# Queries and keys in blocks of 256 tokens, empty products first, and the order of the pieces as a table

## The chip, the cores and the metric

The kernel runs on one core of a Trainium2 chip. The core has five engines that each work off a queue of their own, in order: TensorE (PE, with its weight loads PEld), VectorE (DVE), ScalarE (ACT), GpSimd (POOL) and SyncE (SP), which here issues all DMA transfers. Sixteen DMA engines move the data. The metric is the device time of one execution in microseconds (us), as the median of several runs; lower is better.

## What is computed

Two layers follow each other. The first is attention with 8 heads of 64 on 4 sequences of 768 tokens. A token sees the 8 first tokens and the last 96, with a bias that falls with distance by a slope of its own for each head. Its output, 512 wide, goes into a mixture of 4 attention experts; each has its own projections, a causal attention over the whole sequence, and a gate that keeps the best two experts of each token.

```python
def _attn_ref(q, k, v, n_global, n_local) -> np.ndarray:
    B, H, S, D = q.shape
    scale = 1.0 / np.sqrt(D)
    scores = scale * np.matmul(q, k.transpose(0, 1, 3, 2))
    pos = np.arange(S)
    rel = pos[:, None] - pos[None, :]
    is_global = pos[None, :] < int(n_global)
    is_local = (rel >= 0) & (rel < int(n_local))
    keep = is_global | is_local
    dist = np.where(is_global & ~is_local, float(n_local), np.abs(rel).astype(np.float32))
    slopes = 2.0 ** (-8.0 * (np.arange(H, dtype=np.float32) + 1) / H)
    bias = -slopes[:, None, None] * dist[None, :, :]
    scores = scores + bias[None, :, :, :]
    scores = np.where(keep, scores, -1000000000.0)
...
    return np.matmul(a, v).astype(np.float32)
...
    for e in range(E):
        q = x @ wq[e]
        k = x @ wk[e]
        v = x @ wv[e]
        scores = scale * (q @ k.transpose(0, 2, 1))
        causal = np.triu(np.ones((S, S), dtype=bool), 1)
        scores = np.where(causal, -1000000000.0, scores)
...
        ye = a @ v @ wo[e]
        for kk in range(K):
            mask = topk[:, :, kk] == e
            out += mask[..., None] * w[:, :, kk:kk + 1] * ye
```

## The kernel before

The 4 sequences are cut into 24 units of 128 tokens, six to a sequence (`unit(u)`, u from 0 to 23). A unit is a chain of small pieces, each a function that emits a few instructions on one engine; the pieces' names are short and come back in the rows below by the tiles that they write.

First attention. `ldq`, `ldk`, `ldv` (L519) load 128 tokens of each input as 32-bit numbers into `raw`, 256 KB a load; a token's 64 numbers of one head are 256 bytes in one piece. `cq`, `ck`, `cv` (POOL, by the helper `copy`, L358) make 16-bit numbers of them. `tq` (L536) turns queries and keys by 8 transposes on PE, `eq` (DVE) copies them out of PSUM into `qkT`. `s0`, `s1` (L559) are the scores of four heads each against the unit's own and the previous 128 tokens, with keys along the partitions; `x0`, `x1` (ACT, L563) take the exponential, `m0`, `m1` (DVE, L568) multiply by a table `M` that holds bias and mask, `z0`, `z1` (PE, L576 and L579) form the weighted sum with a column of ones for the denominator, and `r` and `n` (DVE, L590, L592) divide. The 8 global keys and values are put over the first 8 rows of the previous tile's keys and values when that tile's own turn is over: `kg`, `kp` (tiles `KG`, `qkT`) and `vg`, `vp` (a small DMA, L600).

Experts. `tx` and `ex` turn the result; `pq` (L618) and `pv` (L624) project it to queries and keys of all experts and to values and gate; `eqk` copies the first out of PSUM into `QK2`, `ev` the values into `V2`; `xr`, `mx`, `wr`, `zi` make the gate. `s2` (L658) and `x2` (ACT, L662) are the scores and exponentials against all tiles so far, `af` (POOL, L670) the causal mask of the newest, `y2` (L682) the weighted sum, `rz`, `cw` (L689), `n2` the division and the gate, `tz`, `ez`, `po` (L705) the output projection, `eo` its copy out of PSUM and `so` (L714) the store of 256 KB.

Buffers are rings: four for `raw`, three for the 16-bit copies, four for most others. PSUM is shared out as two places for scores (`s`) and four for everything else (`w`), and a piece that writes PSUM takes a place from the readers that were there before.

The order on all queues is made when the program is built: `Stream.run` takes, again and again, the piece that a small cost model lets start first, with a rank for each kind of piece (`RANK`) that rises by `PACE` from unit to unit. Pieces that two engines can do (`eqk`, `ev`, `eo`, `m0`, `m1`, `kg`, the weight casts) go to the one that it finds cheaper. At the end a few sums (`good0` to `flag`) look whether all denominators are in range; a general path follows that isn't taken here.

Of the kernel before, what the change touches and what calls it, by code (L numbers as in the profile page):

```python
# [15 lines left out]
HUGE = 1.0e30  # L16
P = 128
N_G, N_L = 8, 96

PACE, ALPHA, TURN = 6.00622, 0.000375979, 0.1
OTHER = {"m0": 3.12, "m1": 3.35, "eqk": 1.71, "ev": 14.02, "eo": 5.29, "kg": -15.22, "kp": 7.23}
RANK = {
# [8 lines left out]
}  # L33
W_RANK = -47.481, 2.337, 16.829, -53.198, 17.758
# [219 lines left out]
class Stream:  # L254
# [4 lines left out]
    def __init__(self, kinds):  # L259
        self.free = {"PE": 0.0, "ACT": 0.0, "DVE": 0.0, "POOL": 0.0, "DMA": 0.0}  # L260
        self.tail = {"PE": 0.20, "ACT": 0.15, "DVE": 0.12, "POOL": 0.10, "DMA": 2.0}
        self.kinds = {k: [()] * n for k, n in kinds.items()}
        self.rows = False
        self.ops, self.done, self.slot = {}, {}, None

    def add(self, key, fn, engines, after=(), rank=0.0, kind=None, until=(), rows=False, stage=None):


        assert key not in self.ops, key
        self.ops[key] = (fn, engines, tuple(after), rank, kind, tuple(until), rows, stage)  # L270

    def ready(self, key):
        fn, engines, after, rank, kind, until, rows, stage = self.ops[key]
        t = 0.0
        for a in after:
            if a not in self.done:
                return None
            t = max(t, self.done[a])
        if kind:

            for r in until:
                if any(a not in self.done for a in self.ops[r][2] if a != key and a not in until):
                    return None
            free = [(max([self.done[a] for a in r], default=0.0), n)
                    for n, r in enumerate(self.kinds[kind]) if all(a in self.done for a in r)]
            if not free:
                return None
            when, self.slot = min(free)
            t = max(t, when)
        return t  # L290

    def run(self):
        left = dict.fromkeys(self.ops)
        while left:
            best = None
            for key in left:
                t = self.ready(key)
                if t is None:
                    continue
                fn, engines, after, rank, kind, until, rows, stage = self.ops[key]  # L300
                for n, (e, length) in enumerate(engines.items()):
# [3 lines left out]
                    if best is None or c < best[0]:  # L305
                        best = c, start, key, e, length, self.slot
# [6 lines left out]
            if e == "PE":  # L313
                self.rows = rows
# [479 lines left out]
```

## Time and profile before

| | |
|---|---|
| median of 3 runs | 157.07 us (156.87 to 157.64) |
| the profiled execution | 157.58 us |
| its span, first to last instruction | 155.8 us |
| DVE busy | 126.7 us (81% of the span) |
| PE busy | 124.4 us (80%) |
| ACT busy | 111.0 us (71%) |
| POOL busy | 72.0 us (46%) |
| DMA engines, the main queue's packets | 77.7% of sixteen engines' span |

The span is what the trace shows; the time of an execution is a little longer, because something lies before the first and after the last instruction. Busy time counts the union of an engine's records. Records of neighbouring instructions overlap a little, so the sum of the records of an engine can be more than its busy time. The PE's ends are modelled, and PE is pipelined, so a busy PE need not be at its peak.

### The profile page before, as it was taken

The numbers are of one execution on the slowest core, as the hardware profiler recorded it, in microseconds if no ns is written. First come the engines' busy times: TensorE is split into PE (matmuls) and PEld (weight loads), VectorE is DVE, ScalarE is ACT, GpSimd is POOL, SyncE is SP. The second block draws the span as 40 slices with busy tenths as digits, with TensorE's granted clock in tenths as the row PEclk, the third lists the DMA queues.
The fourth block names the chain that finished last, engine by engine and source line by source line (L and its number), as shares of the span: only waits on it lengthen the run. The fifth ranks groups of instructions, "written<-read, shape, count | busy, mean of one in ns | idle before, by whom it ended". The sixth has DMA issues, their size and how long they took to land.

```text
span 155.8 us, 5666 instructions
## 1 busy us (share of the span) xinstructions
PE 124.4 (80%) x2246; PEld 99.6 (64%) x2246; DVE 126.7 (81%) x438; ACT 111.0 (71%) x186; POOL 72.0 (46%) x132
## 2 busy tenths in 40 slices
PE   0027885959888988998899989999699999999820
PEld 0015774737777767985777876867588788777400
DVE  3228678987999999898899999999699999978710
ACT  4902457646867987889499968996478879999810
POOL 5037433636476655557938465654392321221000
PEclk9999999999999999999999999999999999999985
DMA  2999669899997999998997999995990221232550
GB/s 52 315 222 215 180 201 231 166 203 234 222 215 137 207 251 217 212 199 172 260 230 206 224 232 199 265 210 144 221 186 4 76 76 67 74 135 74 196 208 13
DMA packets 80687, 27.85 MB, mean 179 GB/s; under 512 B 75632, under 2 KB 77328, under 8 KB 80656
## 3 DMA queue, kind: packets, MB, share of 16 engines
q1 hardware_dynamic: 80656, 27.45, 77.7%
q8 instruction: 18, 0.29, 0.9%
q14 instruction: 13, 0.11, 0.3%
HBM read 20.98 MB, written 6.29 MB: 175 GB/s over the span
## 4 chain that ended last, share of the span: by engine, by line
PE 35%; DVE 21%; DMA 20%; POOL 6%; ACT 5%; issue 5%; SPq 4%; POOLq 0%; ACTq 0%; DVEq 0%
DMA raw<-in_q_dram 13%; DMA raw<-in_k_dram 7%; PE pq L618 6%; DVE A L568 5%; POOL qk L358 5%; PE tq L536 5%; PE po L705 4%; PE z L682 4%; PE s L658 4%; DVE qkT L358 4%; PE pv L624 3%; ACT A L563 3%; PE sc L559 3%; DVE QK L358 2%; DVE cw L689 2%
## 5 line engine op out<-in xcount | busy, mean ns | idle before, releaser
L563 ACT ACTIVATE A<-sc 128x1024 f16<-128x1024 f32 (+1 forms) x48 | 44.8, 962 | 16.0 <-PE sc L559 15.8
L662 ACT ACTIVATE A<-s 128x1024 f16<-128x1024 f32 (+1 forms) x48 | 44.0, 929 | 9.1 <-PE s L658 9.0
L358 POOL CAST qk<-raw 128x512 f16<-128x512 f32 x47 | 31.4, 671 | 31.2 <-DMA raw<-in_q_dram 19.2
L568 DVE TENSOR_TENSOR A<-A,M 128x1024 f16<-128x1024 f16 (+1 forms) x48 | 32.8, 690 | 1.6 <-ACT A L563 1.4
L536 PE MATMUL tq<-ident,qk 128*128 128x128 f16 x192 | 16.1, 231 | 16.3 <-POOL qk L358 15.8
L618 PE MATMUL pq<-xT,wqk 128*128 128x128 f16 x384 | 26.2, 223 | 0.9 <-DVE xT L358 0.7
L670 POOL TENSOR_SCALAR_AFFINE_SELECT A<-A 128x512 f16<-128x512 f16 x24 | 16.8, 699 | 18.8 <-ACT A L662 17.7
L618 PEld LDWEIGHTS <-wqk 128*128 128x128 f16 x384 | 23.1, 100 | 2.6 <-issue 0.9
L536 PEld LDWEIGHTS <-qk 128*128 128x128 f16 x192 | 12.2, 103 | 19.3 <-POOL qk L358 18.1
L358 POOL CAST V<-raw 128x512 f16<-128x512 f32 x24 | 16.2, 675 | 12.2 <-DMA raw<-in_v_dram 6.8
L358 DVE COPY qkT<-tq 128x1024 f16<-128x1024 f16 x24 | 16.3, 678 | 4.1 <-PE tq L536 3.9
L576 PE MATMUL z<-V,A 128*128 128x65 f16 x192 | 17.7, 198 | 2.3 <-POOL V L358 0.9
L592 DVE TENSOR_TENSOR x<-z,rall 128x256 f16<-128x256 f32 x48 | 19.2, 412 | 0.0
L358 DVE CAST QK<-pq 128x512 f16<-128x512 f32 x24 | 16.3, 680 | 1.6 <-PE pq L618 1.6
L658 PE MATMUL s<-QK 64*128 64x128 f16 x336 | 16.2, 218 | 1.3 <-DVE QK L358 1.1
L559 PE MATMUL sc<-qkT 64*128 64x128 f16 x192 | 15.2, 226 | 1.9 <-DVE qkT L358 1.0
L576 PEld LDWEIGHTS <-A 128*128 128x128 f16 x192 | 13.7, 100 | 3.8 <-DVE A L568 1.2
L358 ACT COPY o_sb<-po 128x512 f32<-128x512 f32 x24 | 14.4, 606 | 2.2 <-PE po L705 1.3
L579 PE MATMUL z<-V,A 128*128 128x65 f16 x160 | 14.9, 195 | 0.1
L624 PE MATMUL pv<-wvg,xT 128*128 128x264 f16 x96 | 14.8, 276 | 0.0
L559 PEld LDWEIGHTS <-qkT 64*128 64x128 f16 x352 | 10.9, 97 | 5.9 <-issue 2.8
L705 PE MATMUL po<-wo,zT 128*128 128x512 f16 x48 | 14.3, 380 | 0.3 <-DVE zT L358 0.2
(57 smaller groups left out, 197.9 us busy)
## 6 DMA issues: line engine op xcount, KB each, us to landing
raw<-in_k_dram SPq DMA_DIRECT2D x24, 256.0 KB
raw<-in_q_dram SPq DMA_DIRECT2D x24, 256.0 KB
raw<-in_v_dram SPq DMA_DIRECT2D x24, 256.0 KB
out_dram<-o_sb SPq DMA_DIRECT2D x24, 256.0 KB
w<-in_moe_wq_dram SPq DMA_DIRECT2D x1, 512.0 KB
w<-in_moe_wk_dram SPq DMA_DIRECT2D x1, 512.0 KB
w<-in_moe_wv_dram SPq DMA_DIRECT2D x1, 512.0 KB
wo<-in_moe_wo_dram SPq DMA_DIRECT2D x1, 512.0 KB
```

Of the source, the lines that this page charges most:

```text
L358: act.copy(o, i) if e == "ACT" else (dve if e == "DVE" else pool).tensor_copy(o, i)
L536: nc.tensor.transpose(ps[:, s, p, :], qk16[u % 3][:, s, 2 * p:2 * p + 2, :], ident[:, :])
L559: mm(sc[:, par, pr, prev * P:(prev + 1) * P], lhsT=kt, rhs=qkT[i][L, 0, p, :], start=True, stop=True)
L563: act.activation(A1[(2 * u + hf) % (2 * R)][:, :, :, 0:w], T.pop(("s", u, hf))[:, :, :, 0:w], func=Exp, scale=scale1)
L568: eng[e].tensor_tensor(a, a, M[:, hf, :, :, :] if ri else M0[:, hf, :, :, :], op=Alu.mult)
L576: mm(z[:, h % 4, :], lhsT=a[:, par, pr, 0:P], rhs=V1[i][:, h, 0:DV], start=True, stop=not ri)
L592: add(f"n{hf}", lambda e, hf=hf, r1=r1: dve.tensor_tensor(x16[i][:, 256 * hf:256 * hf + 256].rearrange("p (h d) -> p h d", d=Dh), T.pop((" ...
L618: mm(ps[:, j, :], lhsT=wqk[:, ko, j, :], rhs=xT[i][:, ko, :], start=(ko == 0), stop=(ko == nko - 1))
L624: mm(ps[:, :], lhsT=xT[i][:, ko, :], rhs=wvg[:, ko, :], start=(ko == 0), stop=(ko == nko - 1))
L658: mm(sc[:, par, n, :], lhsT=QK2[b % 2][L, ki, 2 + p2, :], rhs=QK2[b % 2][L, ri, p2, :], start=True, stop=True)
L662: act.activation(A2[i][:, :, 4 * ch:4 * ch + m, :], T.pop(("s2", u, ch))[:, :, 0:m, :], func=Exp, scale=scale2)
L705: mm(ps[:, :], lhsT=zT[i][:, p2, :], rhs=wo[:, p2, :], start=(p2 == 0), stop=(p2 == E // 2 - 1))
```

## The change

Queries and keys are loaded in blocks of 256 tokens, two units at a time. In a partition lie two neighbouring tokens, so that a piece of a load is 512 bytes: 12 loads of 512 KB for queries and 12 for keys in place of 24 and 24 of 256 KB. Values stay as they were. There are three buffers for blocks.

The cast of the queries sorts the two tokens apart; the cast of the keys interleaves the pair, so that two 16-bit numbers make one 32-bit word. Queries are turned by 8 transposes of 16-bit numbers a block, keys by 4 transposes of 32-bit words (`tk`). The query order inside a tile is now all even tokens and then all odd ones; the tables `d` and `M` are built in that order, and `tx` multiplies by a permutation (`perm`) instead of the identity, which puts the tokens back.

Ahead of everything on PE stand 24 products of 128 by 512 zeros (`warm`), whose result is not read.

The planner is gone. `ORDER` is a table of all pieces in the source. A number behind a colon is the PSUM place; a star means the second of the engines that a piece allows. By its stars, `eqk` goes to ACT in 20 of 24 units (before: DVE in all), `ev` to DVE in 7 and `eo` to DVE in 5 (before: ACT in all), and the casts of the first three weights go to ACT (before: DVE). `kg` is on POOL (before: DVE), and the first block's casts are on ACT and DVE.

```diff
+N_WARM = 24
+ORDER = """
+ident nil ldq-0 warm:2 ldk-0 ident32 ldq-2 dg ldk-2 iota d mask ldv-0 d0 d1 M-1-1 ldq-4 cq-0 ck-0
+ld-k M-0-0 M-1-0 tk-0:3 cq-2 tq-0:1 ek-0 ld-q M-0-1 V1one* eq-0 tq-2:2 perm kg-0 s0-0:1 ldv-1 eq-2
...
     def run(self):
...
+        for word in ORDER.split():
+            name, _, slots = word.partition(":")
+            key = names[name.rstrip("*")]
+            fn, engines, after, kind, until = self.ops[key]
+            assert key not in done and done.issuperset(after), word
+            self.slots = [int(n) for n in slots]
+            assert len(self.slots) == len(until), word
+            for n, readers in zip(self.slots, until):
+                assert done.issuperset(self.kinds[kind][n]), word
+                self.kinds[kind][n] = readers
+            fn(list(engines)[name.endswith("*")])
+            done.add(key)
...
+    RB = 3
+    rawqk = ring(RB, [P, 2, H, 2, Dh], F32, "rawqk")
+    rawv = ring(R, [P, H, Dh], F32, "rawv")
+    q16 = ring(RB, [P, 2, H, Dh], FH, "q16")
+    k16 = ring(RB, [P, H, Dh, 2], FH, "k16")
+    qT = ring(RB, [P, H // 2, 2, P], FH, "qT")
+    kT = ring(RB, [P, H // 2, 2, P], FH, "kT")
...
+    def warm(e):
+
+        ps = wtile([P, 4 * P], F32, "warm")
+        for n in range(N_WARM):
+            mm(ps[:, :], lhsT=nil[:, 0:P], rhs=nil[:, :], start=True, stop=True)
...
+        if u == u0:
+            for n, src in enumerate((q, k)):
+                add("ld" + "qk"[n], lambda e, n=n, src=src: nc.sync.dma_start(
+                    rq[:, n, :, :, :].rearrange("p h j d -> p h (j d)"),
+                    src[b, :, ri * P:(ri + 2) * P, :].rearrange("h (p j) d -> p h (j d)", j=2)),
+                    {"DMA": 1.85}, [("c" + "qk"[n], u - 2 * RB)])
+            add("cq", lambda e: copy(e, q_[:, :, :, :], rq[:, 0, :, :, :].rearrange("p h j d -> p j h d")),
+                {"POOL": 0.99} if u else {"ACT": 0.95}, ["ldq", ("tq", u - 2 * RB)], port=True)
+            add("ck", lambda e: copy(e, k_[:, :, :, :].rearrange("p h d j -> p h j d"), rq[:, 1, :, :, :]),
+                {"POOL": 1.27} if u else {"DVE": 0.75}, ["ldk", ("tk", u - 2 * RB)], port=True)
...
+            def tk(e):
+                T["tk", u] = ps = wtile([P, H // 2, P], F32, "tk")
+                for p in range(H // 2):
+                    nc.tensor.transpose(ps[:, p, :], k_[:, 2 * p:2 * p + 2, :, :].rearrange(
+                        "p h d j -> p (h d j)").bitcast(F32), ident32[:, :])
...
-                nc.tensor.transpose(ps[:, ko, :], xv[:, ko, :], ident[:, :])
+                nc.tensor.transpose(ps[:, ko, :], xv[:, ko, :], perm[:, :])
```

The numbers in braces are lengths that the table's author gave the pieces; nothing reads them any more.

On SP's queue the first loads were those of the gate and query weights, then keys and queries of single units (`raw`); before:

```order
L459 DMA wg_68<-in_moe_w_gate_dram 128x16
L459 DMA w_66<-in_moe_wq_dram 128x4x256
L519 DMA raw_82<-in_k_dram 128x8x64
L459 DMA w_66<-in_moe_wk_dram 128x4x256
L519 DMA raw_82<-in_q_dram 128x8x64
L519 DMA raw_83<-in_k_dram 128x8x64
L519 DMA raw_83<-in_q_dram 128x8x64
L519 DMA raw_82<-in_v_dram 128x8x64
```

and after, with blocks of two units (`rawqk`):

```order
L578 DMA rawqk_85<-in_q_dram 128x8x128
L578 DMA rawqk_85<-in_k_dram 128x8x128
L578 DMA rawqk_86<-in_q_dram 128x8x128
L578 DMA rawqk_86<-in_k_dram 128x8x128
L609 DMA rawv_88<-in_v_dram 128x8x64
L578 DMA rawqk_87<-in_q_dram 128x8x128
L512 DMA w_69<-in_moe_wk_dram 128x4x256
L512 DMA w_69<-in_moe_wq_dram 128x4x256
```

The weights have moved behind the first four units' queries and keys, and queries stand ahead of keys.

PE's queue began with the transposes of the first unit (one row of eight is shown of each piece), its scores, and those of the second unit; before:

```order
L536 LDWEIGHTS qk_0_86
L536 MATMUL tq<-ident,qk_0_86 128x128
L559 LDWEIGHTS qkT_89
L559 MATMUL sc<-qkT_89 128x128
...
L536 LDWEIGHTS qk_1_87
L536 MATMUL tq<-ident,qk_1_87 128x128
```

and after (24 empty products, 4 wide transposes, 8 narrow ones of the first block, 8 of the second block, then scores):

```order
L493 LDWEIGHTS nil
L493 MATMUL warm<-nil 128x512
L596 MATMUL tk<-ident_66,k_0_95 128x128 x4
L591 LDWEIGHTS q_0_92
L591 MATMUL tq<-ident,q_0_92 128x2x64
L591 LDWEIGHTS q_1_93
L591 MATMUL tq<-ident,q_1_93 128x2x64
L630 LDWEIGHTS kT_101
L630 MATMUL sc<-qT_98,kT_101 128x128
```

The second block's query transposes stand ahead of the first scores.

On ACT, after the first exponentials of the experts (tile `A<-s`), there stood only exponentials, the value casts (`V`), the cast of the last weights and the output copies (`o_sb`); before:

```order
L662 ACTIVATE A_0_117<-s_359 128x2x256
L563 ACTIVATE A_5_102<-sc 128x1024
L563 ACTIVATE A_4_101<-sc 128x1024
L637 ACTIVATE el_125<-pv 128x4
L358 CAST wo<-wo_67 128x1024
L358 CAST V_0_115<-pv 128x4x64
```

and after:

```order
L731 ACTIVATE A_0_128<-s_458 128x2x256
L634 ACTIVATE A_6_114<-sc 128x1024
L634 ACTIVATE A_0_108<-sc 128x1024
L634 ACTIVATE A_1_109<-sc 128x1024
L384 CAST QK_0_124<-pq 128x512
L384 CAST wo<-wo_70 128x1024
L708 ACTIVATE el_137<-pv 128x4
```

The cast of the projected queries and keys (`QK`) has come onto ACT's queue, from DVE's.

## Rows read from the trace of the kernel before

**Rows 1.** The page's first part: busy us (share of the span) xinstructions.

```profile
PE 124.4 (80%) x2246; PEld 99.6 (64%) x2246; DVE 126.7 (81%) x438; ACT 111.0 (71%) x186; POOL 72.0 (46%) x132
```

**Rows 2.** ACT by stretches: from:to, us, busy us (x), PEclk, DMA share, GB/s.

```profile
0.00:12.70 12.70, 5.44 (x18) 1.00 0.94 198
12.70:30.00 17.30, 9.96 (x15) 1.00 0.86 194
30.00:117.00 87.00, 67.12 (x105) 1.00 0.99 211
117.00:149.80 32.80, 28.44 (x51) 1.00 0.27 100
```

**Rows 3.** DVE by stretches.

```profile
30.00:117.00 87.00, 80.57 (x262) 1.00 0.99 211
117.00:148.50 31.50, 27.86 (x119) 1.00 0.26 93
```

**Rows 4.** PE by stretches.

```profile
10.40:20.70 10.30, 8.37 (x92) 1.00 1.03 218
...
117.00:149.20 32.20, 31.29 (x567) 1.00 0.27 98
```

**Rows 5.** First 24 us in order: start, us, engine, line, what [idle before <-releaser].

```profile
0.93 0.39 SPq L459 DMA_DIRECT2D wg<-in_moe_w_gate_dram  x1
...
1.37 0.42 SPq L459 DMA_DIRECT2D w<-in_moe_wq_dram  x1
...
5.88 0.69 DVE L358 CAST wqk<-w 128x1024 f16<-128x1024 f32 x1 [2.32 <-DMA w<-in_moe_wq_dram]
...
6.96 0.43 DVE L358 CAST qk<-raw 128x512 f16<-128x512 f32 x1 [0.39 <-DMA raw<-in_k_dram]
...
8.54 0.69 DVE L358 CAST wqk<-w 128x1024 f16<-128x1024 f32 x1 [1.15 <-DMA w<-in_moe_wk_dram]
...
9.77 0.61 POOL L358 CAST qk<-raw 128x512 f16<-128x512 f32 x1 [6.55 <-DMA raw<-in_q_dram]
...
10.44 1.04 PE L536 MATMUL tq<-ident,qk 128*128 128x128 f16 x8 [10.44 <-POOL qk L358]
...
12.70 1.09 ACT L563 ACTIVATE A<-sc 128x512 f16<-128x512 f32 x2 [5.14 <-PE sc L559]
...
17.25 1.86 PE L618 MATMUL pq<-xT,wqk 128*128 128x128 f16 x16 [0.52 <-DVE xT L358]
...
23.04 1.05 PE L618 MATMUL pq<-xT,wqk 128*128 128x128 f16 x16
```

**Rows 6.** Groups by shape: busy us, mean ns | idle before, releaser.

```profile
L358 POOL CAST qk<-raw 128x512 f16<-128x512 f32 x47 | 31.4, 671 | 31.2 <-DMA raw<-in_q_dram 19.2 <-DMA raw<-in_k_dram 12.0
...
L592 DVE TENSOR_TENSOR x<-z,rall 128x256 f16<-128x256 f32 x48 | 19.2, 412 | 0.0
...
L358 DVE CAST QK<-pq 128x512 f16<-128x512 f32 x24 | 16.3, 680 | 1.6 <-PE pq L618 1.6
...
L358 ACT COPY o_sb<-po 128x512 f32<-128x512 f32 x24 | 14.4, 606 | 2.2 <-PE po L705 1.3 <-ACT V L358 0.5 <-ACT o_sb L358 0.4
...
L358 ACT CAST V<-pv 128x256 f16<-128x256 f32 x24 | 9.2, 386 | 1.1 <-DVE mx L640 1.0
...
L689 DVE SCALAR_TENSOR_TENSOR cw<-wr,zi,rall 128x4 f32<-128x4 f32 x24 | 7.3, 303 | 0.1
...
L358 DVE COPY KG<-qkT 128x32 f16<-128x32 f16 x4 | 1.7, 429 | 0.1
...
L358 ACT CAST wo<-wo 128x1024 f16<-128x1024 f32 x1 | 1.1, 1067 | 0.0
...
L742 PE MATMUL pf<-ones,good 128*1 128x1 f32 x6 | 0.3, 163 | 0.0
```

**Rows 7.** The tile cw: its product, ns min/median/max.

```profile
L689 DVE SCALAR_TENSOR_TENSOR cw<-wr,zi,rall x24: 193/220/1219, 27.4 to 147.1; 128x4 f32<-128x4 f32 x24
```

More of the change, by code (lines that the diff above doesn't have):

```diff
@@ L259, in __init__, with add @@
     def __init__(self, kinds):
-        self.free = {"PE": 0.0, "ACT": 0.0, "DVE": 0.0, "POOL": 0.0, "DMA": 0.0}
-        self.tail = {"PE": 0.20, "ACT": 0.15, "DVE": 0.12, "POOL": 0.10, "DMA": 2.0}
         self.kinds = {k: [()] * n for k, n in kinds.items()}
-        self.rows = False
-        self.ops, self.done, self.slot = {}, {}, None
-    def add(self, key, fn, engines, after=(), rank=0.0, kind=None, until=(), rows=False, stage=None):
+        self.ops, self.slots = {}, []
+    def add(self, key, fn, engines, after=(), kind=None, until=(), rows=False, port=False):
@@ L269, in add @@
         assert key not in self.ops, key
[L270 to L290, printed above, removed]
@@ L292, in run @@
-    def run(self):
[L293 to L301, printed above, removed]
-                    turn = TURN if e == "PE" and rows != self.rows else 0.0
-                    start = max(t, self.free[e] + turn)
-                    c = start + OTHER.get(stage, 0.0) * n + ALPHA * rank
-                    if best is None or c < best[0]:
-                        best = c, start, key, e, length, self.slot
-            assert best, list(left)[:20]
-            start, key, e, length, slot = best[1:]
-            fn, engines, after, rank, kind, until, rows, stage = self.ops[key]
-            if kind:
-                self.kinds[kind][slot] = until
-                self.slot = slot
-            if e == "PE":
-                self.rows = rows
-            self.free[e] = start + length
-            self.done[key] = start + length + self.tail[e]
-            del left[key]
-            fn(e)
@@ new lines, in add @@
+        self.ops[key] = (fn, engines, tuple(after), kind, tuple(map(tuple, until)))
+    def run(self):
+        names = {"-".join(map(str, k)) if isinstance(k, tuple) else k: k for k in self.ops}
+        done = set()
+        for word in ORDER.split():
[10 more added lines that the diff above has]
+            done.add(key)
+        assert len(done) == len(self.ops)
@@ new lines @@
+    st.add("dg", c_dg, {"POOL": 0.45})
+    st.add("mask", c_mask, {"POOL": 0.9}, ["d"])
+    st.add("d0", dmin(d0[:, :], d[:, 0:P]), {"DVE": 0.35}, ["mask", "dg"])
+    st.add("d1", dmin(d[:, P:2 * P], d[:, P:2 * P]), {"DVE": 0.35}, ["mask", "dg"])
+    for hf in range(2):
+        st.add(("M", 0, hf), c_factor(True, hf), {"ACT": 0.8}, ["d0"])
+        st.add(("M", 1, hf), c_factor(False, hf), {"ACT": 1.25}, ["d1"])
+    st.add("V1one", fill([t[:, :, Dh:DV + 1] for t in V1], 1.0), {"DVE": 0.3, "POOL": 0.3})
@@ L458, in ld @@
+    st.add("V2one", fill([t[:, :, :, Hd:DV] for t in V2], 1.0), {"DVE": 0.3, "POOL": 0.3})
+    st.add("ones", fill([ones[:, :]], 1.0), {"DVE": 0.1})
     def ld(o, i):
@@ L500, in unit, with add @@
         n_ch = (len(ent) + 3) // 4
-        def add(name, fn, engines, after=(), stage=None, kind=None, until=(), rows=False):
+        def add(name, fn, engines, after=(), kind=None, until=(), rows=False, port=False):
             def full(a):
@@ L508, in add @@
                                             (isinstance(x, tuple) and isinstance(x[1], int) and x[1] < u)],
-                   PACE * u + RANK[stage or name], kind, [full(a) for a in until], rows,
-                   stage or name)
+                   kind, [[full(a) for a in one] for one in until], rows, port)
         def c(key):
```

226 lines of the change are left out of this document (144 added, 82 removed), and 8 rows, old and new, of the table RANK.

## The prediction

> **What bounds the kernel now.** I read the busy line of the page first, then each engine's busy time by stretches, then the groups by shape, and the first 24 us instruction by instruction. The page [rows 1] shows no engine at its limit for the whole span: DVE is busy 126.7 us of 155.8, PE 124.4, ACT 111.0. The stretches say why [rows 2 to 4]. From 30 to 117 us the DMA engines are full (share 0.99), and there DVE, the fullest engine, is busy 80.57 us of 87.00, or 93%, ACT only 67.12, or 77%. From 117 on the DMA share is 0.26, since the loads are over, and PE is busy 31.29 of 32.20 us: it works off the second attention that has been left behind. Before 30 us all of them starve: ACT has its first exponential at 12.70 us [rows 5] and is busy 9.96 of the next 17.30 us. So three things set the end, one after the other: a late and thin start, a middle that is held by loads and nearly as much by DVE, and a last stretch on PE.
>
> **The start.** In order of issue before: gate weights, query weights, keys, key weights, queries of the first tile. The query weights (512 KB, pieces of 1 KB) are issued at 1.37 and used at 5.88; then the keys (256 KB, pieces of 256 B) 1.08 us later, the key weights 1.58 us later, the queries 1.23 us later, at 9.77 [rows 5]. So 256 KB in pieces of 256 B cost about 1.15 us (18 ns for each piece and engine, 1024 pieces on 16 engines), and 512 KB in pieces of 1 KB 1.58 us (49 ns a piece). A block of 256 tokens is 512 KB in pieces of 512 B, and no load here has that size. From above it costs 2 x 1.15 = 2.30 us (no gain from the longer piece), from below 1.58 us. On the line between the two pieces one of 512 B takes 28 ns, which makes 1.82 us; I take that, because both ends come from the same queue within 4 us of each other.
> Now the first queries go first: issued at 0.93, where the queue's first load stands [rows 5], 4.5 us from issue to use as the query weights took, 0.24 us more for the smaller pieces, so 5.7 us; the first keys 7.5, the second block's queries 9.3. PE's own queue puts the transposes of that second block's queries ahead of the first scores, so the first scores wait for them: 9.3 + 1.2 to 1.34 us of POOL cast (the cast of half the size takes 0.67 [rows 6]) + 0.6 + 0.3 of PE gives a first exponential at about **11.6 us**, against 12.70. At the upper price of the loads it would be 13.1.
> The 24 empty products need only a memset and lie ahead of everything on PE. What columns cost is seen at 16 products of 128: 1.86 us at 17.25 and 1.05 us at 23.04 [rows 5], 116 and 66 ns each. Four times these bounds the 24 at 6.3 to 11.2 us, so they end between about 8 and 12.5 us; I take 9, as they come without gaps. Up to there they are hidden behind loads that PE waits for anyway; at 12.5 the first exponential would come near 14.5. The granted clock reads 1.00 (the 2.4 GHz level) in the first stretch of PE's work too [rows 4], though the same products take nearly twice as long there as later; PE had done nothing for ten microseconds before it. I go by the durations. PE is busy 8.37 us from 10.40 to 20.70 [rows 4]; at the later price that is 4.7 us, so the warm start takes some 3.6 us off PE, most of it under other engines' waits.
>
> **What each engine has to do.** Counted in the code's tables: of 24 casts of the second attention's queries and keys (QK, 128x512) 20 go from DVE to ACT; 7 value casts and 5 output copies go from ACT to DVE; three weight casts go from DVE to ACT, the four small key copies (KG) from DVE to POOL.
> DVE: 20 x 0.68 off; 7 x about 0.41 (a DVE operation on 256 columns from PSUM) and 5 x 0.68 on; weights 3 x 0.69 and KG 1.7 off; the first key cast and a memset 0.5 on. Together -13.6 + 2.9 + 3.4 - 2.1 - 1.7 + 0.5 = -10.6, so 116.1 us [rows 1, 6]. The 24 copies of the transposed tiles (12 + 12 instead of 24) keep their size and cost.
> ACT: 20 x 0.61 on (the price of the output copy, the same 128x512 from PSUM), 7 x 0.39 and 5 x 0.61 off, 3 x 1.07 of weight casts and one query cast of 1.07 on: 12.2 - 2.7 - 3.1 + 4.3 = +10.7, so **121.7 us** [rows 1, 6]. ACT becomes the fullest engine, and the fullest engine of all falls by only 126.7 - 121.7 = 5.0 us: balance alone gives no more.
> PE: per block 16 transposes of 128 columns become 8, and 4 of 32-bit words. A 32-bit transpose isn't in the trace; the only 32-bit products are recorded as two each (6 for 3 calls) [rows 6]. Eight narrow ones take 1.04 us at 10.44 [rows 5], 0.6 at the later price. Below, 4 wide ones cost as much as 4 narrow (0.3 us); above, four times that, 1.2 us. Against the 8 that they replace this is -0.3 to +0.6 us a block, -3.6 to +6.6 us in 12 blocks; two passes each, as the recorded ones, make 0.6 and no change. I take 0.
> POOL: 47 casts of 0.67 (31.4 us) become 22 of twice the size. At twice the price 29.5 us; the key cast writes every second element, which I bound at one to two times that (29.5 to 44). POOL is busy 72.0 us now and has room. What it can cost is DVE's time: DVE's small product cw takes 193 ns at best and 1219 at worst [rows 7], 303 in the mean [rows 6]. I read the excess, 24 x 0.11 = 2.6 us, as DVE waiting for POOL. Half as many casts of twice the length cover the same time, but each hit lasts twice as long, so the part that the casts cause, 31.4 of POOL's 72.0 us [rows 1, 6], doubles: 1.2 us more on DVE; 0 if the new order keeps the two apart.
> The Trainium skill says the same in its page "SBUF — State Buffer", section "SBUF: two separate sides": the pair of ports that DVE and GpSimd share is an exclusive lock, held for the whole instruction, and the loser blocks fully. By that rule alone the longer casts speak against the change; the worst row [rows 7] agrees, at 1.0 us over the best. What that would make of the time is the rival on POOL's casts below.
> DMA: the loads of queries and keys fall from 48 x 1.15 = 55 us to 24 x 1.82 = 44, so 11.5 us of a stretch that was full until 117 [rows 2]; at the ends of the price 0 to 17. The queue of SP also loses 24 load instructions, but its order is fixed, and a load behind a store that waits for ACT waits too.
>
> **The sum**, along ACT, against the profiled execution's span. First exponential at 11.6. Of ACT's 121.7 us, 5.44 lie before it [rows 2] and 1.07 of query cast: 115.2 remain. Its records overlap a little with their neighbours, so 20 added casts count for about 1 us less: 114.2. The last stretch stays what it was, 28.44 us of work in 32.80 [rows 2], because it hangs on the chain of each last tile and on PE. The other 85.8 us run at the share that the fullest engine reached before, 80.57 of 87.00 [rows 3]: 92.6 us. Then 6.0 us from ACT's last copy to the end (149.80 to 155.80). 11.6 + 92.6 + 32.8 + 6.0 = 143.0. The median stands 157.07 - 155.8 = 1.3 us above the span (the profiled execution itself, 157.58, 1.8). **Forecast 144.3 us.**
> Two checks. DVE: first copy at about 9.6, 116.1 - 1.8 (set-up ahead of it) + 1.2 = 115.5 of work, idle 3.6 in the last stretch (27.86 of 31.50 [rows 3]) and some 4 elsewhere, 7.3 after it: 140.0. PE: from 9, 124.4 - 3.6 = 120.8, idle 5, 6.6 after it: 141.4. All three lie within 3 us of each other, so none of them alone decides, and a saving on one shows little.
>
> **The rivals.**
> *Dense table* (17%). A written order may feed ACT better than 93% without load waits: at 98%, as any engine would with full queues, the middle takes 87.6 us, and the last stretch loses half of its 4.4 idle us: 137.1. For it: the DMA is no longer full. Against it: DVE and PE are as loaded.
> *Three full engines in lockstep* (14%). Each queue is in order; where ACT, DVE and PE all need over 115 us, each waits for the others. At 87% the middle takes 98.6 us: 150.3. The wide or slow 32-bit transposes (+6.6 on PE) and a cold first 10 us (+2.9) lead to the same place.
> *The loads still pace* (6%). If a piece of 512 B costs as much as two of 256 (2.30 us a block), the loads end where they did, and the last stretch follows from 117: up to 157, which is no change; with half of it 152. Against it: 1.58 us for pieces of 1 KB [rows 5].
> *Slower: DVE behind POOL's longer casts* (5%). One mechanism: 24 cw and 48 mask products meet casts of 1.3 us. If each waited 0.3 us more than now (a hit of 1 us, as the worst one shows [rows 7], in every third), DVE has 72 x 0.3 = 22 us more and the check on DVE gives 140.0 + 22 + 1.3 = 163. It decides from 0.23 us on each, 17 us in all. The same row speaks against: median 220 ns against a best of 193, so most meet nothing.
> *It doesn't do what it says* is inside these: if the empty products leave PE no faster, 147.
>
> **How the numbers follow.** Forecast 58%, 140 to 148. Dense 17%, stalls 14%, loads 6% (half of them within 0.5% of 157.07, half faster), POOL 5%. A measurement of this kernel can tell about 0.5% from no change. Faster 0.92, within 0.5% 0.03, slower 0.05. The range leaves out the lowest 5% or so of the dense case and, above, half of the load case, the POOL case and the worst stalls: 138 to 151.
>
> **What would show it.** In the profile after: ACT busy near 121 us and the fullest or next to it, QK casts on ACT at 0.6; DVE near 116; the first exponential at 11 to 12; 16 products of a query and key projection at about 1.0 us from the first; a DMA share clearly under 0.99 in the middle, and loads that end ahead of 110; four 32-bit transposes within 0.6 us. Wrong would be: a middle where ACT is under 87% busy, waits of the score products or of DVE for POOL of over 10 us, a share of 0.99 again, or cw over 500 ns in the mean.

## The result, and the profile after

The changed kernel takes 146.50 us in the median of 4 runs (146.05 to 146.97), against 157.00 before (4 runs, 156.87 to 157.64): a ratio of 0.932, 95% interval 0.929 to 0.936. In a second comparison, beside the experiments, it was 146.34 (ratio 0.923, 0.914 to 0.933). The forecast was 144.3 with a range of 138 to 151; the sign and the range held, and the time is 2.2 us longer than forecast. The kernel before came out at 157.0 to 158.7 in the different comparisons, so each experiment is given with its own ratio to it. Some executions of a kernel, profiled ones among them, fall into a second state that is some per cent slower; medians are of all runs, the ratios of the fast runs alone.

The first part of the page after (busy us, share of the span of 144.9, instructions), then the granted clock and the DMA share by fortieths of the span, the main DMA queue (packets, MB, share of sixteen engines) and the shares of the chain that ended last:

```profile
PE 130.0 (90%) x2222; PEld 101.5 (70%) x2222; DVE 120.2 (83%) x420; ACT 120.1 (83%) x198; POOL 70.2 (48%) x116
...
PEclk9999555999999999999999999999999999999999
DMA  2999999599898997969999699770527204023164
...
q1 hardware_dynamic: 55696, 27.45, 72.2%
...
PE 60%; DVE 14%; DMA 8%; SPq 7%; issue 3%; ACT 2%; POOL 2%; ACTq 0%
```

Against [rows 1] ACT has gained 9.1 us of work (forecast 10.7) and DVE has lost 6.5 (forecast 10.6). PE's 130.0 hold 7.0 us of empty products; without them it has 123.0, 1.4 less than before. The DMA queue moves the same 27.45 MB in 72.2% x 144.9 = 104.6 us of sixteen engines, where it took 77.7% x 155.8 = 121.1.

ACT by stretches (from:to, us, busy us (instructions), granted clock, DMA share, GB/s), the answer to [rows 2]:

```profile
0.00:10.72 10.72, 6.39 (x18) 1.00 0.90 219
10.72:30.00 19.28, 12.60 (x16) 0.73 0.96 254
30.00:117.00 87.00, 80.62 (x128) 1.00 0.81 205
30.00:131.00 101.00, 93.35 (x150) 1.00 0.73 187
131.00:139.90 8.90, 7.01 (x16) 1.00 0.19 71
```

And the same of DVE (first fence) and PE (second fence), the answers to [rows 3] and [rows 4]:

```profile
30.00:98.00 68.00, 63.97 (x207) 1.00 0.94 234
30.00:117.00 87.00, 82.27 (x278) 1.00 0.81 205
30.00:131.00 101.00, 94.34 (x328) 1.00 0.73 187
```

```profile
8.50:30.00 21.50, 15.56 (x208) 0.76 0.99 256
8.50:15.00 6.50, 4.01 (x63) 1.00 1.19 294
15.00:25.00 10.00, 7.92 (x81) 0.50 1.02 253
30.00:117.00 87.00, 84.35 (x1579) 1.00 0.81 205
30.00:131.00 101.00, 98.35 (x1854) 1.00 0.73 187
```

Between 30 and 117 us ACT was busy 77% and is now 93%; DVE went from 93% to 95%, and the DMA engines from 0.99 to 0.81, because most of their work ends earlier: up to 98 us the share is still 0.94, then the DMA row falls to 0. The last load of queries or keys is issued at 85.40 us (before at 110.08); only the last three value loads come after 98 us, the last of them at 109.81. All three engines run at 92 to 97% up to 131 us, and PE has no backlog of the second attention to work off alone: only the last ten microseconds of ACT's work, from 131 us to its last copy's end at 140.7, are thin. The gain lies in the middle; the start is 2 us better, and the end stays an end.

The first 30 us (start, us, engine, line, what), as in [rows 5]:

```profile
1.35 7.02 PE L493 MATMUL warm<-nil 128*128 128x512 f16 x24 [1.35 <-DVE nil L479]
...
6.89 0.77 DVE L384 CAST k<-rawqk 128x1024 f16<-128x1024 f32 x1 [2.61 <-DMA rawqk<-in_k_dram]
...
8.21 0.60 PE L596 MATMUL tk<-ident,k 128*128 128x128 f32 x4
...
8.75 1.04 POOL L384 CAST q<-rawqk 128x1024 f16<-128x1024 f32 x1 [4.81 <-DMA rawqk<-in_q_dram]
...
10.59 1.33 POOL L384 CAST k<-rawqk 128x1024 f16<-128x1024 f32 x1 [0.24 <-DMA rawqk<-in_k_dram]
...
10.72 1.08 ACT L634 ACTIVATE A<-sc 128x512 f16<-128x512 f32 x2 [1.30 <-PE sc L630]
...
18.08 0.69 DVE L384 CAST wvg<-wg 128x16 f16<-128x16 f32 x2 [0.69 <-DMA wg<-in_moe_w_gate_dram]
...
20.17 1.90 PE L689 MATMUL pq<-xT,wqk 128*128 128x128 f16 x16
...
28.84 1.07 PE L689 MATMUL pq<-xT,wqk 128*128 128x128 f16 x16 [1.18 <-DVE z L761]
```

The empty products end at 8.4, and the clock falls all the same: its row reads 1.00 (2.4 GHz) to 15 us, 0.50 (1.2 GHz) from 15 to 25, and 1.00 from there on. The 16 products of the first projection still take 1.90 us, as before.

### The profile page after: what moved, and what is told of

The parts are those of the page before. It is cut to its first block, busy times and chain, and to the rows that moved or that the text cites. A ratio compares the mean times of both kernels' runs of the same rounds, so it can differ in the third digit from the quotient of the medians.

```text
span 144.9 us, 5515 instructions
## 1 busy us (share of the span) xinstructions
PE 130.0 (90%) x2222; PEld 101.5 (70%) x2222; DVE 120.2 (83%) x420; ACT 120.1 (83%) x198; POOL 70.2 (48%) x116
## 3 DMA queue, kind: packets, MB, share of 16 engines
q1 hardware_dynamic: 55696, 27.45, 72.2%
## 4 chain that ended last, share of the span: by engine, by line
PE 60%; DVE 14%; DMA 8%; SPq 7%; issue 3%; ACT 2%; POOL 2%; ACTq 0%
PE pq L689 13%; PE s L727 7%; PE sc L630 7%; PE pv L695 6%; PE z L647 5%; PE z L751 5%; DMA wg<-in_moe_w_gate_dram 5%; PE po L774 4%; SPq L578 4%; DMA rawqk<-in_k_dram 4%; PE tx L679 3%; PE tk L596 3%; DVE A L639 3%; PE z L650 3%; PE tq L591 3%
## 5 line engine op out<-in xcount | busy, mean ns | idle before, releaser
L639 DVE TENSOR_TENSOR A<-A,M 128x1024 f16<-128x1024 f16 (+1 forms) x48 | 35.0, 742 | 0.2 <-ACT A L634 0.2
L384 POOL CAST k<-rawqk 128x1024 f16<-128x1024 f32 x11 | 15.3, 1388 | 12.7 <-DMA rawqk<-in_k_dram 12.6
L630 PE MATMUL sc<-qT,kT 64*128 64x128 f16 x352 | 17.4, 224 | 2.5 <-DVE kT L384 1.2
L647 PE MATMUL z<-V,A 128*128 128x65 f16 x192 | 17.1, 196 | 2.2 <-POOL V L384 1.0
L384 POOL CAST V<-rawv 128x512 f16<-128x512 f32 x24 | 15.7, 658 | 3.9 <-PE s L727 1.9
L647 PEld LDWEIGHTS <-A 128*128 128x128 f16 x192 | 13.1, 99 | 5.1 <-DVE wr L712 0.8
L384 POOL COPY kT<-KG 128x32 f16<-128x32 f16 x20 | 5.4, 272 | 20.9 <-PE sc L630 20.9
L630 PEld LDWEIGHTS <-kT 64*128 64x128 f16 x352 | 11.1, 97 | 5.9 <-issue 1.9
L384 POOL CAST q<-rawqk 128x1024 f16<-128x1024 f32 x11 | 11.7, 1059 | 6.7 <-DMA rawqk<-in_q_dram 6.7
L650 PE MATMUL z<-V,A 128*128 128x65 f16 x160 | 14.6, 195 | 0.0
L384 ACT CAST QK<-pq 128x512 f16<-128x512 f32 x20 | 11.9, 595 | 2.5 <-PE pq L689 2.5
L751 PE MATMUL z<-V,A 128*128 128x65 f16 x336 | 13.8, 193 | 0.0
L751 PEld LDWEIGHTS <-A 128*128 128x128 f16 x336 | 12.3, 97 | 1.8 <-issue 0.4
```

Of the source, the lines that this page charges most:

```text
L384: act.copy(o, i) if e == "ACT" else (dve if e == "DVE" else pool).tensor_copy(o, i)
L630: mm(sc[:, par, pr, prev * P:(prev + 1) * P], lhsT=share(kT, u - prev)[L, p, :], rhs=share(qT, u)[L, p, :], start=True, stop=True)
L639: eng[e].tensor_tensor(a, a, M[:, hf, :, :, :] if ri else M0[:, hf, :, :, :], op=Alu.mult)
L647: mm(z[:, h % 4, :], lhsT=a[:, par, pr, 0:P], rhs=V1[i][:, h, 0:DV], start=True, stop=not ri)
L751: mm(z[:, ex, :], lhsT=A2[i][:, ex % 2, n, :], rhs=V2[b % 2][:, ki, ex, 0:DV], start=(j == 0), stop=(j == len(mine) - 1))
```

## The experiments

Two theories stood at the start. The one of the prediction: more room in the DMA and the shift from DVE to ACT give the gain together, and ACT, DVE and PE then end within 3 us of each other. Rivals: the warm start gives a part of it; the loads' piece size gives nearly all of it; one engine alone is the new bound.

**Without the empty products** (one is left of 24).

```diff
-N_WARM = 24
+N_WARM = 1
```

> The changed kernel with 1 empty product instead of 24 (all else as it is, 146.5 us). Theory (the empty products buy a fast start, but the clock falls back at about 15 us in any case): the first block's transposes and scores take twice as long, first exponential at 11.5 to 12.5 instead of 10.72, the time 147.3 to 148.5. Rival A (nothing is bought, because the clock was at the lower level from 15 to 25 us anyway): 146.1 to 146.9. Rival B (the products at the start only bring a fall at 15 us; without them the clock rises at about 20 us as in the kernel before): 144.5 to 145.8.

Measured: 147.16 us (146.08 to 148.21), ratio 0.931 (0.919 to 0.942), which can't be told from the changed kernel's; it lies between the ranges of the theory and of rival A. The first query transposes and the first projection in this run:

```profile
8.68 2.20 PE L591 MATMUL tq<-ident,q 128*128 128x128 f16 x16
...
20.86 1.90 PE L689 MATMUL pq<-xT,wqk 128*128 128x128 f16 x16
```

The first query transposes take nearly twice as long each here (16 in 2.20 us, against 8 in 0.61 after), so the empty products do speed up PE up to 15 us; the first exponential comes at 11.25 instead of 10.72. Nothing of it is seen at the end.

**More empty products**, 18 in seven groups where PE waits between 11 and 21 us.

```diff
+MORE = {"f0": 2, "f1": 1, "f2": 1, "f3": 3, "f4": 4, "f5": 5, "f6": 2}
...
+    for name, n in MORE.items():
+        st.add(name, more(n), {"PE": 0.215 * n}, ["nil"], "w", [[]])
```

> The changed kernel with 18 more empty products, in 7 groups of 1 to 5, at the places between 11 and 20 us where PE waits. Theory (the ten microseconds at the lower clock level, 15 to 25 us, are dear, because every engine hangs on PE there): the granted clock stays at 1.00 past 15 us, ACT is busy 2 to 4 us more of 10.7 to 30, the time 142.5 to 144.5. Rival (the start is paced by loads and small waits, or the empty products hold up the pieces behind them): 146.0 to 147.5, also where the clock stays up.

Measured: 147.57 us (145.79 to 149.05), ratio 0.925 (0.914 to 0.936). PE in this run from 15 to 20 us, and its first projection:

```profile
15.00:20.00 5.00, 4.21 (x36) 1.00 0.95 259
```

```profile
21.36 1.06 PE L700 MATMUL pq<-xT,wqk 128*128 128x128 f16 x16
```

The clock stays at 1.00 in every fortieth of the span and the 16 products take 1.06 us instead of 1.90, and still the time is the same. Three kernels with three clocks in the first 30 us, one time: PE's clock there is worth less than these comparisons resolve, some 2 us by their intervals. Why is not shown; it may be that until 30 us the engines wait for loads, casts and each other more than for PE. This run is also no clean test of the clock, since its 18 products take time on PE in the same stretch, and its first 24 end at 9.46 us instead of 8.37.

**The empty products alone**, ahead of the kernel before.

```diff
+    def warm(e):
+        ps = wtile([P, 4 * P], F32, "warm")
+        for n in range(24):
+            mm(ps[:, :], lhsT=nil[:, 0:P], rhs=nil[:, :], start=True, stop=True)
```

> The kernel before with only the 24 empty products put at the front of PE's queue (the rest in the same order). Theory (PE's first ten microseconds of work at the lower level cost about 3.6 us of PE, most of it under other waits): 155 to 156.3. Rival (PE idles between the end of the empty products at 8.4 and the first transposes at 10.4 and then works thinly, so that the clock falls again before it helps): 156.5 to 157.5.

Measured: 156.48 us (155.87 to 157.69), ratio 0.988 (0.979 to 0.998). So in the kernel before they gave 0.3 to 3.3 us by the interval, which doesn't decide between theory and rival; the first exponential came at 11.73 instead of 12.70.

**Pieces of 256 bytes again**: the same blocks, tiles and order, but a block's load is two loads that each bring every second token.

```diff
-                add("ld" + "qk"[n], lambda e, n=n, src=src: nc.sync.dma_start(
-                    rq[:, n, :, :, :].rearrange("p h j d -> p h (j d)"),
...
+                add("ld" + "qk"[n], lambda e, n=n, src=src: [nc.sync.dma_start(
+                    rq[:, n, :, j, :],
...
+                    for j in range(2)],
```

> The changed kernel with each load of queries or keys as two loads of 256 KB in pieces of 256 B, the same bytes into the same places. Theory (the longer piece is what makes room on the DMA engines): first exponential 1.0 to 1.5 us later, DMA share of the main queue from 72% to about 80%, more waits of POOL for keys and queries than 19 us, the time 148 to 150.5. Rival (the loads don't pace the new order, only the number of bytes counts): 146.1 to 147.2.

Measured: 156.33 us (154.70 to 157.54), ratio 0.985 (0.975 to 0.996): nearly all of the gain is gone, far more than the theory's 148 to 150.5. Its main queue, then ACT from 30 to 117 us, then what PE and POOL waited for longest (us in total, times, longest):

```profile
q1 hardware_dynamic: 80656, 27.45, 77.0%
```

```profile
30.00:117.00 87.00, 72.55 (x112) 0.98 0.89 202
```

```profile
PE tk L597 <- POOL k L384: 7.0, 7, 2.7
```

```profile
POOL k L384 <- DMA rawqk<-in_k_dram: 20.6, 9, 5.0
...
POOL q L384 <- DMA rawqk<-in_q_dram: 11.8, 7, 6.4
```

In the changed kernel POOL waits 12.6 and 6.7 us for the same loads and PE 0.4 for POOL's keys. The chain is plain: loads, POOL's casts, PE's transposes, and ACT falls from 80.62 to 72.55 us of work in 87. The queue's time is 77.0% x 155.8 = 120.0 us, against 104.6. The Trainium skill, page "DMA: Bandwidth & Descriptors", section "Specifications", gives 512 bytes as the smallest transfer for line rate. The runs agree nearly: the shorter pieces cost 15 us more of the queue's time for the same 27.45 MB, and by the packet records of the kernel after, the median piece takes 18 ns at 256 bytes, 27 at 512 and 49 at 1 KB, so 512 bytes come within a tenth of the rate of 1 KB. One thing isn't told apart: this kernel also issues 24 loads more than the changed one, and the price of those is within the 9 to 10 us.

**All QK casts back on DVE** (20 of them from ACT; all 20 stars, one row is shown).

```diff
-m1-3 eqk-1* tq-6:1 tx-2:0 m1-4 w-o z0-3:2 ex-2 s20-1:1 r0-3 s0-5:0 m0-4 pq-2:0 xr-1 x0-5 wr-1 eq-6
+m1-3 eqk-1 tq-6:1 tx-2:0 m1-4 w-o z0-3:2 ex-2 s20-1:1 r0-3 s0-5:0 m0-4 pq-2:0 xr-1 x0-5 wr-1 eq-6
```

> All 24 QK casts go to DVE again (20 come back from ACT), in the changed kernel's order otherwise: DVE gets 20 x 0.60 = 12 us more, ACT 12 us less. Theory (DVE's work is paid in full, as its doubled copies showed with +6.6 for +6.7): +9 to +12, a ratio to the kernel before of 0.99 to 1.01, and DVE busy 130 to 132. Rival (PE sets the pace, and the relief of ACT gives most of it back): +3 to +6, a ratio of 0.95 to 0.97.

Measured: 155.85 us (155.26 to 156.39), ratio 0.987 (0.977 to 0.997): +9.4, as the theory said, with a ratio a little under its 0.99. The page's busy line and its chain:

```profile
PE 133.1 (86%) x2222; PEld 102.4 (66%) x2222; DVE 131.1 (85%) x440; ACT 112.4 (73%) x178; POOL 69.1 (45%) x116
...
DVE 51%; PE 37%; issue 3%; ACT 3%; POOL 3%; DVEq 0%; ACTq 0%
```

DVE's share of the chain goes from 14% to 51%, and from 30 to 131 us DVE is busy 97.48 of 101 us. With the long pieces but without the shift, DVE is the bound; with the shift but without the long pieces (the run above), the loads are. Each of the two alone is worth little: undoing either one costs 9 to 10 us of a gain of 10.5. One thing stays open here: the table's order was made for these places of the casts, and a move in the other direction costs 3 us too (below), so part of the +9.4 may be the price of a disturbed order. What the order by itself is worth against the planner's was not tested.

**What each engine's work costs now.** Three kernels do one kind of operation twice: the 48 key transposes on PE, 17 value casts on ACT, 24 copies of the transposed second attention (`ez`) on DVE.

```diff
-                for p in range(H // 2):
+                for p in [*range(H // 2)] * 2:
```

> The changed kernel with every transpose of the keys done twice (the same result): 48 more 32-bit transposes, in groups of four that take 0.45 us, so PE has about 5.4 us more, of which 4.5 us lie after 30 us. Theory (PE is what bounds it: 78.8 of 80 us busy from 50 to 130): 4 to 5.5 us longer than the changed kernel on the same chip. Rival (ACT bounds it, as the prediction's sum had it, and PE's records only look full): 0 to 2 us longer.

```diff
-        add("ev", lambda e: copy(e, V2[b % 2][:, ri, :, 0:Hd],
-                                 T["pv", u][:, 0:E * Hd].rearrange("p (e d) -> p e d", d=Hd)),
+        add("ev", lambda e: [copy(e, V2[b % 2][:, ri, :, 0:Hd],
+                                 T["pv", u][:, 0:E * Hd].rearrange("p (e d) -> p e d", d=Hd))
+                             for _ in range(2 if e == "ACT" else 1)],
```

> The changed kernel with the 17 value casts on ACT done twice (the same result): ACT has 17 x 0.38 = 6.5 us more. Theory (PE bounds it and ACT has idle time, 7.7 us of it between 30 and 131 us): 1 to 3 us longer. Rival (ACT bounds it): 4.5 to 6.5 us longer.

```diff
-        add("ez", lambda e: copy(e, zT[i][:, :, :], T.pop(("tz", u))[:, :, :]), {"DVE": 0.2},
+        add("ez", lambda e: [copy(e, zT[i][:, :, :], t[:, :, :]) for t in [T.pop(("tz", u))] * 2], {"DVE": 0.2},
```

> The changed kernel with the 24 copies of zT on DVE done twice (the same result): DVE has 24 x 0.28 = 6.7 us more. Theory (PE bounds it and DVE has some idle time, 4.7 us between 30 and 117 us): 1.5 to 4 us longer. Rival (DVE and its waits for POOL bound it): 5 to 7 us longer.

The changed kernel itself ran beside them:

> The changed kernel itself again, as the base for the kernels sent with it. Its ratio to the kernel before was 0.932; both theories expect 0.925 to 0.94.

| | work added | median | against 146.34 | ratio to before |
|---|---|---|---|---|
| unchanged copy | none | 146.34 | | 0.923 (0.914 to 0.933) |
| PE | 48 transposes, 12 x 0.45 = 5.4 | 150.85 | +4.5 | 0.954 (0.946 to 0.962) |
| ACT | 17 x 0.38 = 6.5 | 149.06 | +2.7 | 0.938 (0.930 to 0.946) |
| DVE | 24 x 0.28 = 6.7 | 152.90 | +6.6 | 0.965 (0.957 to 0.974) |

By the medians, the work added on DVE is paid in full, on PE to some 80%, on ACT to some 40%; each difference is uncertain by 1 to 2 us. DVE's price is the clear one, and the theory that PE alone is the bound falls with it; ACT, along which the prediction made its sum, comes out cheapest. PE's price is less certain than it looks: in the profiled execution (149.99 us, the shortest of the four) ACT's last output copy ends at 141.78 us, against 140.69 in the changed kernel and 139.76 in its copy, so 1.1 to 2.0 us later; the rest of its longer span lies behind that, where a last packet of the stores starts late. The page's busy time doesn't help: without any added work, PE's 2222 products are busy 129.6 us in the copy and 132.0 in the DVE run. And each price is that of one kind of operation at its place in the chain; other operations of the same engine were not tried.

**The twelve value casts and output copies back on ACT** (7 `ev`, 5 `eo`; one row is shown): the test in the other direction, relief for DVE.

```diff
-eo-0 cq-8 ex-3 s21-2:1 s0-7:0 rz-1 x21-2 mx-2 pq-3:2 zi-1 ldv-7 cw-1 x0-7 cv-6 ev-2* wr-2 tq-8:0
+eo-0 cq-8 ex-3 s21-2:1 s0-7:0 rz-1 x21-2 mx-2 pq-3:2 zi-1 ldv-7 cw-1 x0-7 cv-6 ev-2 wr-2 tq-8:0
```

> The 7 value casts and 5 output copies that the change put on DVE go back to ACT, in the changed kernel's order otherwise: DVE 7 x 0.41 + 5 x 0.69 = 6.3 us less, ACT 5.6 us more. Theory (DVE's work counts in full, ACT's at about a third): -6.3 + 2.0, so -3 to -4.5, 142 to 143.5. Rival (PE is as full as DVE, so a relief of DVE alone gives little): -1 to +1, 145.5 to 147.5.

Measured: 149.81 us (149.45 to 151.25), ratio 0.953 (0.942 to 0.963): 3 us slower, where the theory had 3 to 4.5 faster and the rival no change. Both fell. The busy line, and what DVE waited for:

```profile
PE 131.3 (89%) x2222; PEld 102.3 (69%) x2222; DVE 112.7 (76%) x408; ACT 124.2 (84%) x210; POOL 71.3 (48%) x116
```

```profile
DVE wr L712 <- ACT V L384: 4.1, 7, 1.5
...
DVE mx L711 <- ACT el L708: 3.0, 4, 1.4
...
DVE mx L711 <- ACT V L384: 2.3, 3, 1.2
DVE wr L712 <- ACT el L708: 2.0, 4, 0.8
```

In the changed kernel the same waits are 1.0, 2.6, none and 0.2 us. So DVE has 7.5 us less to do and waits 7.6 us more for ACT in these rows: the relief is handed straight to a wait. (All its idle time grows by 10.3 us, from 24.7 to 35.0; what makes up the rest is not shown.) `mx` and `wr` are the gate's small operations on DVE; what they wait for on ACT now stands behind, or is, one of the casts that came back. Taking work off DVE by giving it to ACT is thus no test of DVE alone, and a price found by adding work can't be turned round into a gain.

**The same with the gate weights' load first** on SP's queue.

```diff
-ident nil ldq-0 warm:2 ldk-0 ident32 ldq-2 dg ldk-2 iota d mask ldv-0 d0 d1 M-1-1 ldq-4 cq-0 ck-0
+ident nil ld-g ldq-0 warm:2 ldk-0 ident32 ldq-2 dg ldk-2 iota d mask ldv-0 d0 d1 M-1-1 ldq-4 cq-0 ck-0
```

> As e11_evo, and the load of the gate weights (32 KB) stands first on SP's queue, where it stood in the kernel before, and not behind the loads of the first four blocks, where it landed at 18 us. Theory (the chain of the first gate waits for it): another 0.5 to 1.5 us less than e11_evo. Rival (other waits stand behind that one): no difference, 0 +- 0.5.

Measured: 151.37 us (149.41 to 152.78), ratio 0.950 (0.937 to 0.962) against 0.953 without it: no difference that can be told, as the rival said. It tests little, though: in the run without it the cast of the gate weights starts at 17.98 us with no wait before it, so the wait of 0.69 us that the changed kernel shows at 18.08 wasn't there to be won. (The load has 8 KB, not 32.)

**Half of POOL's casts of queries and keys**, from the fourth block on.

```diff
+            hh = H if u < 2 * RB else H // 2
-            add("cq", lambda e: copy(e, q_[:, :, :, :], rq[:, 0, :, :, :].rearrange("p h j d -> p j h d")),
+            add("cq", lambda e: copy(e, q_[:, :, 0:hh, :], rq[:, 0, 0:hh, :, :].rearrange("p h j d -> p j h d")),
...
-            add("ck", lambda e: copy(e, k_[:, :, :, :].rearrange("p h d j -> p h j d"), rq[:, 1, :, :, :]),
+            add("ck", lambda e: copy(e, k_[:, 0:hh, :, :].rearrange("p h d j -> p h j d"), rq[:, 1, 0:hh, :, :]),
```

> From the fourth block on, POOL casts only half of the heads of queries and keys (the other half of these casts is left out of the computation): POOL has 18 casts of half the length, about 11 us less, and DVE, PE and ACT keep all their work. Theory (POOL's long casts cost DVE time through its waiting): the mask products fall from 797 ns in the mean towards 730, DVE's busy time by 2 to 4 us, the time by 1 to 3. Rival (the casts cost DVE nothing and PE doesn't wait for them): 0 +- 0.7.

Measured: 144.80 us (143.67 to 145.85), ratio 0.915 (0.905 to 0.926): 1.5 us under the changed kernel by the medians, with intervals that overlap by about half. The mask products here and after by min/median/max (ns), and their mean at the full size (busy us, mean ns), after in the first fence of each pair:

```profile
L639 DVE TENSOR_TENSOR A<-A,M x48: 396/681/1762, 11.3 to 126.0; 128x1024 f16<-128x1024 f16 x40, 128x512 f16<-128x512 f16 x8
```

```profile
L640 DVE TENSOR_TENSOR A<-A,M x48: 393/681/1191, 11.4 to 125.2; 128x1024 f16<-128x1024 f16 x40, 128x512 f16<-128x512 f16 x8
```

```profile
L639 DVE TENSOR_TENSOR A<-A,M 128x1024 f16<-128x1024 f16 x40 | 31.5, 797 | 0.0
```

```profile
L640 DVE TENSOR_TENSOR A<-A,M 128x1024 f16<-128x1024 f16 x40 | 29.8, 754 | 0.0
```

The median stays and the worst falls by 0.57 us. What makes a product long is seen in the changed kernel's own trace, where one begins 0.02 us after a cast on POOL:

```profile
42.33 1.56 DVE L639 TENSOR_TENSOR A<-A,M 128x1024 f16<-128x1024 f16 x1
```

```profile
42.31 1.04 POOL L384 CAST q<-rawqk 128x1024 f16<-128x1024 f32 x1 [0.31 <-DMA rawqk<-in_q_dram]
```

The product ends 0.54 us after the cast. So do the others: of the 40, the 15 that overlap nothing on POOL take 652 to 693 ns, and the eleven over 700 ns all begin while a cast or a causal mask (`af`) is running on POOL and end 0.49 to 0.55 us after it. A product thus waits for what is left of POOL's instruction. The nine that overlap a cast of queries or keys make up 3.3 of the 4.6 us that the 40 take above the median; value casts and POOL's masks make up the rest.

What shorter casts bring is small: 40 x 43 ns = 1.7 us of DVE's time, of which the second profile of the changed kernel (mean 770) leaves 0.6, because value casts and masks then hit more. DVE's busy time is 118.5 us, 1.7 or 0.4 less than in the changed kernel's two profiles, where the theory had 2 to 4. That the kernel is faster by 1 to 3 us is not shown.

## Why the prediction was right, and where not

**The shape was right.** Three limits one after the other; the loads leave the middle, the work goes from DVE to ACT, and ACT, DVE and PE stand together. The two runs that undo one side each (256-byte pieces, QK casts on DVE) show the two limits that the profile before named, 0.99 of the DMA and 93% of DVE: lift one alone and the other one holds nearly the old time.

**The sum along ACT** gave 144.3, and it hides errors that partly cancel:

| term | forecast | measured | difference |
|---|---|---|---|
| first exponential | 11.6 | 10.72 | -0.9 |
| ACT's work from there on | 114.2 | 113.7 | -0.5 |
| ACT's idle time up to its last copy | 6.8 + 4.4 = 11.2 | 6.7 + 7.6 + 1.9 = 16.2 | +5.0 |
| from there to the span's end | 6.0 | 4.2 | -1.8 |
| outside the span | 1.3 | 1.6 | +0.3 |

The idle time is the mis-sized term. It was taken as one share, 93%, from the first exponential on; that share came true from 30 to 117 us (80.62 of 87.00), but the first 19 us after the first exponential run at 65%, 12.60 of 19.28, hardly better than before (9.96 of 17.30). The stage before 30 us should have been a term of its own, as the tail was. That the total came within 2.2 us owes something to luck, since the start, ACT's work and the end of the span were each over-estimated, by 3.2 us together. That the last stretch would stay as it was, 28.44 in 32.80, was wrong too, though it cost the sum little: with the loads out of the way earlier, PE keeps pace with the other engines up to 131 us.

**The start.** The order of the loads did what was forecast: keys used at 6.89 (7.5), the second block's queries at 8.75 (9.3). The empty products end at 8.4 (9). That they "take some 3.6 us off PE" was wrong: they hold the upper level of the clock to 15 us only, PE without them is busy only 1.4 us less than before, the first projection's 16 products took 1.90 us where 1.0 was given as a sign, and the runs with one, with 24 and with 42 take the same time. The remark on the rivals that the time is 147 if the empty products leave PE no faster comes nearest to what was seen.

**DVE and ACT.** ACT's 121.7 came out as 120.1, the moved QK casts at 595 ns each. DVE's 116.1 + 1.2 came out as 120.2, 3 us more. Of that, the mask products account for 2.7 (40 at 797 ns in the mean, 730 before; 1.6 by the second profile's 770), and this is in the main the term of POOL's longer casts, forecast at 1.2: I looked for it at the wrong tile. `cw`, by which it was priced, did not rise at all (mean 269, median 223, worst 975 ns, against [rows 7]). The mask products before, then `cw` after:

```profile
L568 DVE TENSOR_TENSOR A<-A,M 128x1024 f16<-128x1024 f16 x40 | 28.9, 730 | 1.0 <-ACT A L563 0.9
```

```profile
L758 DVE SCALAR_TENSOR_TENSOR cw<-wr,zi,rall x24: 191/223/975, 27.3 to 138.0; 128x4 f32<-128x4 f32 x24
```

The Trainium skill's rule that GpSimd and a DVE operation with two SBUF inputs lock a port pair against each other for the whole instruction (page "SBUF — State Buffer", section "SBUF: two separate sides") is borne out by the overlaps shown for the run with half the casts: the products over 700 ns end 0.49 to 0.55 us after the POOL instruction during which they began. The price that would have made the change slower, 0.23 us on each of 72 operations or 17 us, was not near: the mean rose by 67 ns on the 40 full mask products and fell on the 24 `cw`.

**POOL.** Its 22 casts were forecast at 29.5 to 44 us and came out a little under, at 11 x 1388 + 11 x 1059 ns = 26.9 us: twice the size costs less than double for queries (1059 against 2 x 671) and about double for the interleaved keys.

```profile
L384 POOL CAST k<-rawqk 128x1024 f16<-128x1024 f32 x11 | 15.3, 1388 | 12.7 <-DMA rawqk<-in_k_dram 12.6
...
L384 POOL CAST q<-rawqk 128x1024 f16<-128x1024 f32 x11 | 11.7, 1059 | 6.7 <-DMA rawqk<-in_q_dram 6.7
```

**PE's 32-bit transposes.** Taken at no change against the eight that they replace: four take 0.60 us together at 8.21, and doubling them added 0.43 to 0.48 us in each of the first three blocks. The bound of +6.6 us, four times a narrow one each, was far off; the pass count of the only other 32-bit product in the trace pointed the right way.

**The DMA.** Forecast 11.5 us less of the loads, with ends of 0 and 17; measured 121.1 - 104.6 = 16.5, near the upper end. The price of the new piece was right: its packets take 27 ns in the median (28 forecast, on the line between 18 and 49), and the second block's queries and keys are used 1.86 and 1.84 us after the block loaded just ahead of them, where 1.82 was taken. What was mis-sized is the old loads, priced from the first few alone. Over the whole run a 256-byte packet took 20.4 ns in the mean before, so that 48 loads took 62.7 us of sixteen engines and not 55; a 512-byte packet took 31.7 after, so that 24 blocks took 48.7 and not 44. That is 14.0 us of the 16.5; the rest is mostly value loads and stores, whose packets became a little quicker.

**The rivals.** The dense table (137.1) did not come: ACT stayed at 92 to 93% in the middle, where PE's records fill 97%. The loads would have paced at 152 to 157 had the piece not become cheaper: the run with 256-byte pieces measured 156.3. The lockstep of three full engines (150.3) came in part, as the 5 us of idle time more and as the relief of DVE that ended in a wait for ACT. That none of the three alone decides fits the runs; the choice of ACT for the sum was not a good one: work added on ACT cost some 40% of its length, work added on DVE all of it.

## What to carry to other kernels

Where two limits lie close together (here a full DMA and an engine at 93%), price an edit that lifts both as one thing: undoing either half gave back nearly the whole gain, so the halves must not be added up or tried singly and dropped. Before work is moved between two engines that are both over 90% busy, look at what stands behind it in the receiver's queue and who waits for that, since the giver's relief may come back as a wait of the same size. And doubling one cheap operation on each engine gives a first idea of whose time is paid for, which the busy shares (90, 83 and 83%) did not: DVE's came out dearest and ACT's cheapest. It is a price at that place in the chain, and not one for the whole engine.

## What was not expected of the hardware

The record of the granted clock doesn't tell the first level. With one empty product it reads 1.00 in every fortieth of the span, yet 16 transposes took 2.20 us at 8.68 and 16 projections 1.90 at 20.86, the time that they take after at a recorded 0.50, and 1.8 times the 1.06 of the run with 42 empty products. The clock record in that trace has its first entry at 25.9 us, and the row shows what lies ahead of it as 1.00. In the kernel before the first entry is at 20.9, between the two projections of 1.86 and 1.05 us that the prediction couldn't square with a row of 1.00. Ahead of the first entry durations are to be read, not the row.

The clock's upper level did not last. After 7.0 us of dense products PE was busy 4.01 of the 6.5 us up to 15, with short products and transposes, and then the row fell to 0.50 for ten microseconds. With 18 more products in the gaps it did not fall. In both cases the time was the same.
